# Attention over grouped heads: moving the softmax division from ACT's output pass to POOL

One change to a tuned attention kernel: the division by the softmax row sum, which ScalarE (ACT) did while it took the output out of PSUM, is done later by GpSimd (POOL), from an f32 copy in SBUF. VectorE (DVE) computes the reciprocals for four tiles of 128 rows at a time, and the order of the matmuls on TensorE (PE) changes.

## The chip, the core and the metric

The kernel runs on one core of a Trainium2 chip. The metric is the device time of one execution in microseconds (us). In both kernels PE multiplies and transposes into the memory PSUM, ACT and DVE read PSUM, POOL reads and writes the memory SBUF only, and SP issues the DMAs.

## The reference

```python
B, Hq, Hkv, Sq, Sk, D = 16, 16, 8, 384, 384, 256      # bf16
k = jnp.repeat(k, 2, axis=1); v = jnp.repeat(v, 2, axis=1)
scores = jnp.einsum("bhqd,bhkd->bhqk", q, k) * D ** -0.5
p = softmax(scores, axis=-1)
out = jnp.einsum("bhqk,bhkd->bhqd", p, v)
```

## The kernel before

An *item* is 128 query rows of one key/value head. There are 768 of them, 12 to a *group* (two key/value heads of one batch entry, one set of loads and one store). For each item:

| step | engine | what it does |
|---|---|---|
| S | PE | 2 matmuls, 384 columns: scores into PSUM |
| max | DVE | row maximum of the scores, negated |
| exp | ACT | exp(score - max), bf16, to SBUF |
| T | PE | 3 transposes of 128x128 |
| copy | DVE | transposed weights from PSUM to SBUF |
| PV | PE | 3 matmuls, 257 columns: V has a column of ones, so column 257 is the row sum |
| recip | DVE | 1 / row sum |
| output | ACT | output x reciprocal, bf16, to SBUF |

POOL scales K once for each group. A planner gives every instruction a place in the order of its engine and a semaphore wait for each dependence. The places are set by offsets from a step number `y`. The code is shortened: `...` and the comments in the last loop stand for lines left out.

```python
    A_S = 2            # scores run two items ahead
    D_PV = 2           # PV follows two items later
    D_REC = 3; D_OE = 3
    NSB = 4; NWB = 4   # PSUM banks for scores, and for transposes + output
    ...
        def mk_oe(x):                                   # ACT's output pass
            g, u, t = item_gut(x)
            def emit(eng):
                return eng.activation(
                    out=O_sb[g % NOS][:, u, t, :], in_=O_ps(x)[:, 0:D], func=ACTF.Identity,
                    scale=recip[:, (x % NREC):(x % NREC) + 1])
            return emit
    ...
                    o = pl.add("sp", f"ldkt{g % NGS}", mk_load_kt(g), deps, dma=True, ...)
                    ks = pl.add("pool", "pool_ks", mk_kscale(g), [o], ...)   # at once after the load
    ...
        for y in range(y_min, y_max + 1):
            try_loads(y)
            # x = y + A_S:  pl.add("pe",  ... mk_s(x))
            # x = y - D_PV: pl.add("pe",  ... mk_pv(x))
            # x = y - D_REC: pl.add("dve", ... mk_recip(x))
            # x = y - 1:    pl.add("dve", ... mk_pte(x))     the copy
            # x = y + 2:    pl.add("dve", ... mk_max(x))
            # x = y:        pl.add("act", ... mk_exp(x)); pl.add("pe", ... mk_t(x))
            # x = y - D_OE: pl.add("act", ... mk_oe(x)); store after the last item of a group
```

Of the kernel before, what the change touches and what calls it, by code (L numbers as in the profile page):

```python
# [88 lines left out]
def bass_standalone__gqa_softmax__near_ridge_kernel(  # L89
# [12 lines left out]
    assert Sk * 4 <= 2048, "S tile must fit in one PSUM bank"  # L102
    PT_BYTES = JK * 128 * 2
    assert PT_BYTES % 4 == 0 and PT_BYTES + (D + 1) * 4 <= 2048, "PT + O tile must fit one PSUM bank"
    scale = float(D) ** -0.5
# [9 lines left out]
    NWB = 4  # L115
    A_S = 2
    D_PV = 2
    D_T = 0
    D_REC = 3
    D_PTE = 1  # L120
    A_MAX = 2
    D_OE = 3
    NGS = 4
    NOS = 4
    PF = 20
    NP, NPT, NNEG, NREC = 4, 4, 8, 8
    SPLIT_GROUPS = 2
# [5 lines left out]
    def grp_bk(g):  # L133
        U0 = g * GU
        return U0 // Hkv, U0 % Hkv

    with ExitStack() as es:
        def sb(name, shape, dtype):
            return es.enter_context(nc.sbuf_tensor(name, shape, dtype))

        def ps(name, shape, dtype):
            return es.enter_context(nc.psum_tensor(name, shape, dtype))

# [6 lines left out]
        P_sb = [sb(f"P_sb{i}", [128, Sk], BF16) for i in range(NP)]  # L150
        PT_sb = [sb(f"PT_sb{i}", [128, JK, 128], BF16) for i in range(NPT)]
        negm = sb("negm", [128, NNEG], F32)
        recip = sb("recip", [128, NREC], F32)

        S_ps = [ps(f"S_ps{i}", [128, Sk], F32) for i in range(NSB)]
        W_ps = [ps(f"W_ps{i}", [128, 1024], BF16) for i in range(NWB)]

        def PT_ps(x):
            return W_ps[x % NWB][:, 0:JK * 128].rearrange("p (c n) -> p c n", c=JK)

        def O_ps(x):
            e0 = PT_BYTES // 2
            return W_ps[x % NWB][:, e0:e0 + 2 * (D + 1)].bitcast(F32)

# [10 lines left out]
        def G(key):  # L175
            return ops.get(key)

        def item_gut(x):
            g = x // IPG
            u = (x % IPG) // IPU  # L180
            t = x % IPU
            return g, u, t

        def emit_ones(eng):
# [7 lines left out]
        def mk_vones(i):  # L192
            def emit(eng):
                return eng.memset(V_sb[i][:, :, :, D:D + 1], 1.0)  # L194
            return emit

        def mk_load_kt(g, u0=0, nu=None):
# [49 lines left out]
        def mk_kscale(g, u0=0, nu=None):  # L247
            nu = GU if nu is None else nu

            def emit(eng):  # L250
                kt = KT_sb[g % NGS][:, :, u0 * 128:(u0 + nu) * 128]
                return eng.tensor_scalar(out=kt, in0=kt, scalar1=scale, scalar2=0.0,  # L252
                                         op0=ALU.mult, op1=ALU.add)
            return emit

        def mk_s(x):
            g, u, t = item_gut(x)

            def emit(eng):
                last = None  # L260
                for dc in range(DC):
                    last = eng.matmul(  # L262
                        out=S_ps[x % NSB][:, :],
                        lhsT=QT_sb[g % NGS][:, DC * t + dc, u * 128:(u + 1) * 128],
                        rhs=KT_sb[g % NGS][:, dc:JK * DC:DC, u * 128:(u + 1) * 128],
                        start=(dc == 0), stop=(dc == DC - 1))
                return last
            return emit

        def mk_max(x):  # L270
            def emit(eng):
                return eng.tensor_reduce(  # L272
                    out=negm[:, (x % NNEG):(x % NNEG) + 1], in_=S_ps[x % NSB][:, :],
                    axis=AXL.X, op=ALU.max, negate=True)
            return emit

        def mk_exp(x):
            def emit(eng):
                return eng.activation(  # L279
                    out=P_sb[x % NP][:, :], in_=S_ps[x % NSB][:, :], func=ACTF.Exp,  # L280
                    bias=negm[:, (x % NNEG):(x % NNEG) + 1], scale=1.0)
            return emit

        def mk_t(x):
            def emit(eng):
                last = None
                for kc in range(JK):
                    last = eng.transpose(  # L288
                        out=PT_ps(x)[:, kc, :],
                        in_=P_sb[x % NP][:, kc * 128:(kc + 1) * 128],  # L290
                        identity=ident[:])
                return last
            return emit
# [19 lines left out]

        def mk_recip(x):
            def emit(eng):
                return eng.reciprocal(out=recip[:, (x % NREC):(x % NREC) + 1],  # L316
                                      in_=O_ps(x)[:, D:D + 1])
            return emit

        def mk_oe(x):  # L320
            g, u, t = item_gut(x)

            def emit(eng):
                return eng.activation(  # L324
                    out=O_sb[g % NOS][:, u, t, :], in_=O_ps(x)[:, 0:D], func=ACTF.Identity,
                    scale=recip[:, (x % NREC):(x % NREC) + 1])
            return emit

        def emit_warm(eng):
            last = None  # L330
            for i in range(N_WARM):
                last = eng.matmul(out=S_ps[NSB - 1][:, 0:128], lhsT=ident[:], rhs=ident[:],  # L332
                                  start=True, stop=True)
            return last

# [7 lines left out]
        def last_item_of_group(g):  # L343
            return g * IPG + IPG - 1

        next_load = [0]

        def try_loads(y):
            while next_load[0] < NG:
                g = next_load[0]  # L350
                if y < g * IPG - A_S - PF:
                    return
# [23 lines left out]
                else:  # L376
                    o = pl.add("sp", f"ldkt{g % NGS}", mk_load_kt(g), deps, dma=True, name=f"ldkt{g}")
                    ks = pl.add("pool", "pool_ks", mk_kscale(g), [o], name=f"kscale{g}")
                    o = pl.add("sp", f"ldqt{g % NGS}", mk_load_qt(g), deps, dma=True, name=f"ldqt{g}")
                    for u in range(GU):  # L380
                        ops[("kscale", g, u)] = ks
                        for t in range(IPU):
                            ops[("ldqt", g, u, t)] = o
                    for u in range(GU):
                        ops[("ldv", g, u)] = pl.add("sp", f"ldv{g % NGS}_{u}", mk_load_v(g, u), vdeps, dma=True, name=f"ldv{g}_{u}")
                next_load[0] += 1

        y_min = -A_S - PF
        y_max = NI - 1 + max(D_OE, D_PV, D_T, D_REC, D_PTE) + 1
        for y in range(y_min, y_max + 1):  # L390
            try_loads(y)

            x = y + A_S
            if 0 <= x < NI:
                g, u, t = item_gut(x)
                deps = [ops[("ldqt", g, u, t)], ops[("kscale", g, u)], (G(("exp", x - NSB)), "order"), G("warm")]
                ops[("s", x)] = pl.add("pe", "pe_s", mk_s(x), deps, name=f"s{x}")
            x = y - D_PV
            if 0 <= x < NI:
                g, u, t = item_gut(x)  # L400
                deps = [ops[("pte", x)], ops[("ldv", g, u)]]
                ops[("pv", x)] = pl.add("pe", "pe_pv", mk_pv(x), deps, name=f"pv{x}")

            x = y - D_REC
            if 0 <= x < NI:
                deps = [ops[("pv", x)], (G(("oe", x - NREC)), "order")]
                ops[("recip", x)] = pl.add("dve", "dve_recip", mk_recip(x), deps, name=f"recip{x}")
            x = y - D_PTE
# [12 lines left out]

            x = y - D_T
            if 0 <= x < NI:
                deps = [ops[("exp", x)], (G(("oe", x - NWB)), "order"), ops["ident"]]
                ops[("t", x)] = pl.add("pe", "pe_t", mk_t(x), deps, name=f"t{x}")

            x = y - D_OE
            if 0 <= x < NI:
                g = x // IPG
                deps = [ops[("pv", x)], ops[("recip", x)], (G(("store", g - NOS)), "order")]  # L430
                ops[("oe", x)] = pl.add("act", "act_oe", mk_oe(x), deps, name=f"oe{x}")
                gg, u, t = item_gut(x)
                for pi, (u0, nu, t0, nt) in enumerate(store_pieces(g)):
                    if u == u0 + nu - 1 and t == t0 + nt - 1:
                        deps = [ops[("oe", g * IPG + uu * IPU + tt)]
                                for uu in range(u0, u0 + nu) for tt in range(t0, t0 + nt)]
                        chan = f"st{g % NOS}" if pi == 0 else f"st_last{pi}"
                        o = pl.add("sp", chan, mk_store(g, u0, nu, t0, nt), deps, dma=True, name=f"store{g}_{pi}")
                        if pi == 0:
                            ops[("store", g)] = o  # L440

        for x in range(NI):
            for kname in ("s", "max", "exp", "t", "pte", "pv", "recip", "oe"):
                assert (kname, x) in ops, (kname, x)
# [67 lines left out]
```

## Time and profile before

| | before |
|---|---|
| time, median of 4 | 656.96 us (656.9 to 657.67) |
| span of the profiled execution | 655.2 us |
| time per item in steady state (end of exp to end of exp) | 836.8 ns |
| start of the last exp to the end of the span | 5.1 us |

The first fence holds lines of the profile page of the kernel before: the busy time of each engine with its share of the span, and the chain of waits that ended last. SPq is SP's sequencer, which issues the DMAs, and "issue" is time in which an engine waited for nothing that the profile shows.

```profile
PE 647.8 (99%) x6180; PEld 448.6 (68%) x6180; DVE 643.0 (98%) x2308; ACT 644.8 (98%) x1537; POOL 95.3 (15%) x72
...
ACT 92%; issue 3%; SPq 3%; DMA 1%; PE 0%; DVE 0%
```

Three engines are 98 to 99% busy, so the busy shares don't say which of them sets the pace. The next lines are the costliest groups of the same page. The columns are source line, engine, operation, output<-inputs, shapes and count, then total busy us and mean ns of one, then idle time before it and what ended it.

```profile
L279 ACT ACTIVATE P_sb<-S_ps,negm 128x384 bf16<-128x384 f32 x768 | 542.6, 707 | 5.8 <-DVE negm L272 5.6
L324 ACT ACTIVATE O_sb<-W_ps,recip 128x256 bf16<-128x256 f32 x768 | 465.9, 607 | 1.6 <-DVE recip L316 1.6
L272 DVE TENSOR_REDUCE negm<-S_ps 128x1 f32<-128x384 f32 x768 | 428.3, 558 | 7.4 <-PE S_ps L262 7.3
L297 DVE COPY PT_sb<-W_ps 128x384 bf16<-128x384 bf16 x768 | 259.9, 338 | 0.7 <-PE W_ps L288 0.7
```

The two ACT records together are 1,314 ns for an item that takes 837 ns. Records of one engine overlap: an instruction's record opens while the one before it is still running. So a mean duration is not what an instruction costs its engine, and the distances between instructions must be read. The timeline of ACT in steady state (start us, duration us, engine, line, operation):

```profile
300.40 0.71 ACT L279 ACTIVATE P_sb<-S_ps,negm 128x384 bf16<-128x384 f32 x1
300.86 0.61 ACT L324 ACTIVATE O_sb<-W_ps,recip 128x256 bf16<-128x256 f32 x1
301.23 0.71 ACT L279 ACTIVATE P_sb<-S_ps,negm 128x384 bf16<-128x384 f32 x1
```

From exp to output pass 0.46 us, back to exp 0.37 us. PE at two times, first early in the run (13 us), then in steady state:

```profile
13.00 0.33 PE L288 MATMUL W_ps<-ident,P_sb 128*128 128x128 bf16 x3
13.16 0.49 PE L262 MATMUL S_ps<-KT_sb,QT_sb 128*128 128x384 bf16 x2
13.49 0.50 PE L306 MATMUL W_ps<-V_sb,PT_sb 128*128 128x257 bf16 x3
13.82 0.33 PE L288 MATMUL W_ps<-ident,P_sb 128*128 128x128 bf16 x3
...
300.33 0.34 PE L288 MATMUL W_ps<-ident,P_sb 128*128 128x128 bf16 x3
300.50 0.49 PE L262 MATMUL S_ps<-KT_sb,QT_sb 128*128 128x384 bf16 x2
300.83 0.50 PE L306 MATMUL W_ps<-V_sb,PT_sb 128*128 128x257 bf16 x3
301.16 0.34 PE L288 MATMUL W_ps<-ident,P_sb 128*128 128x128 bf16 x3
```

Early on, an item takes 827 ns and every matmul follows the one before at once. Later it takes 837 ns, and the transposes begin 56 ns after exp has ended (at 301.11: 300.40 + 0.71), item after item. In between, exp's records grow by about 10 ns per item. ACT is the slower of the two, by that much; when a load stall has let it catch up, PE shows its own pace for some 15 items.

### The profile page before, as it was taken

The page shows a single profiled execution, that of the slowest core. Times are in us where ns is not written, and L with a number is a line of the kernel's source. Part 1 is how long each engine was busy: PE and PEld are TensorE (multiplying, and loading weights), DVE is VectorE, ACT ScalarE, POOL GpSimd, SP SyncE. Part 2 cuts the span into 40 slices and gives each one's busy share as a digit, 9 for nine tenths or more (in the row PEclk, how much of TensorE's full clock was granted, in tenths as well). Part 3 has the DMA queues.
Part 4 walks back from the last instruction along what each step waited for, and adds up shares of the span by engine and source line. Part 5 has one row for each costly group of instructions (what it writes and reads, how often), then busy time and mean ns, then how long its engine had stood idle before and what let it go on. Part 6 is the DMA issues. An engine that isn't in the chain of part 4 may idle for free.

```text
span 655.2 us, 16888 instructions
## 1 busy us (share of the span) xinstructions
PE 647.8 (99%) x6180; PEld 448.6 (68%) x6180; DVE 643.0 (98%) x2308; ACT 644.8 (98%) x1537; POOL 95.3 (15%) x72
## 2 busy tenths in 40 slices
PE   7999999999999999999999999999999999999997
PEld 6777666666666666666666666666666666666665
DVE  5999999999999999999999999999999999999997
ACT  5999999999999999999999999999999999999998
POOL 1111111101101101101111110110110111101100
PEclk9999999999999999999999999999999999999999
DMA  8999999999999999999999999999999999999932
GB/s 153 171 256 221 254 258 241 261 253 258 214 245 248 232 244 250 218 262 250 230 251 255 233 258 250 246 233 253 243 237 235 227 253 221 227 249 247 225 126 98
DMA packets 368019, 152.11 MB, mean 232 GB/s; under 512 B 302272, under 2 KB 351680, under 8 KB 367936
## 3 DMA queue, kind: packets, MB, share of 16 engines
q1 hardware_dynamic: 367936, 151.02, 104.2%
q8 instruction: 49, 0.80, 0.5%
q14 instruction: 34, 0.28, 0.2%
HBM read 25.17 MB, written 50.33 MB: 115 GB/s over the span
## 4 chain that ended last, share of the span: by engine, by line
ACT 92%; issue 3%; SPq 3%; DMA 1%; PE 0%; DVE 0%
ACT P_sb L279 54%; ACT O_sb L324 38%; SPq L203 1%; SPq L214 1%; DMA QT_sb<-in_q_dram 1%; SPq L223 0%; DVE negm L272 0%; PE W_ps L306 0%; PE S_ps L262 0%; DVE PT_sb L297 0%; PE W_ps L288 0%; DVE recip L316 0%
## 5 line engine op out<-in xcount | busy, mean ns | idle before, releaser
L279 ACT ACTIVATE P_sb<-S_ps,negm 128x384 bf16<-128x384 f32 x768 | 542.6, 707 | 5.8 <-DVE negm L272 5.6
L324 ACT ACTIVATE O_sb<-W_ps,recip 128x256 bf16<-128x256 f32 x768 | 465.9, 607 | 1.6 <-DVE recip L316 1.6
L272 DVE TENSOR_REDUCE negm<-S_ps 128x1 f32<-128x384 f32 x768 | 428.3, 558 | 7.4 <-PE S_ps L262 7.3
L306 PE MATMUL W_ps<-V_sb,PT_sb 128*128 128x257 bf16 x2304 | 382.4, 274 | 0.1
L262 PE MATMUL S_ps<-KT_sb,QT_sb 128*128 128x384 bf16 x1536 | 375.1, 326 | 2.1 <-DMA QT_sb<-in_q_dram 1.9
L306 PEld LDWEIGHTS W_ps<-V_sb,PT_sb 128*128 128x128 bf16 x2304 | 226.2, 98 | 108.5 <-DVE PT_sb L297 0.4
L297 DVE COPY PT_sb<-W_ps 128x384 bf16<-128x384 bf16 x768 | 259.9, 338 | 0.7 <-PE W_ps L288 0.7
L288 PE MATMUL W_ps<-ident,P_sb 128*128 128x128 bf16 x2304 | 259.3, 221 | 0.8 <-ACT P_sb L279 0.8
L288 PEld LDWEIGHTS W_ps<-ident,P_sb 128*128 128x128 bf16 x2304 | 132.8, 97 | 90.0 <-ACT P_sb L279 1.7
L252 POOL TENSOR_SCALAR KT_sb<-KT_sb 128x1536 bf16<-128x1536 bf16 (+1 forms) x66 | 94.6, 1434 | 526.1 <-DMA KT_sb<-in_k_dram 526.1
L316 DVE RECIPROCAL recip<-W_ps 128x1 f32<-128x1 f32 x768 | 121.2, 158 | 0.5 <-PE W_ps L306 0.5
L262 PEld LDWEIGHTS S_ps<-KT_sb,QT_sb 128*128 128x128 bf16 x1536 | 117.9, 98 | 3.4 <-DMA QT_sb<-in_q_dram 2.9
L332 PE MATMUL S_ps<-ident 128*128 128x128 bf16 x36 | 4.0, 310 | 1.4 <-POOL ident L188 1.4
L332 PEld LDWEIGHTS S_ps<-ident 128*128 128x128 bf16 x36 | 3.8, 145 | 1.4 <-POOL ident L188 1.4
L279 ACT ACT_TABLE_LOAD x1 | 1.3, 1283 | 0.8 <-PEq L497 0.8
L194 DVE MEMSET V_sb<- 128x6 bf16 x4 | 0.2, 63 | 0.9 <-PEq L497 0.9
L188 POOL TENSOR_SCALAR_AFFINE_SELECT ident<-ones_t 128x128 bf16<-128x128 bf16 x1 | 0.3, 293 | 0.1
L185 POOL MEMSET ones_t<- 128x128 bf16 x1 | 0.2, 205 | 0.3 <-POOLq L497 0.3
L497 POOL MEMSET const-float32-0.0<- 128x1 f32 x1 | 0.1, 99 | 0.3 <-issue 0.3
L497 POOL MEMSET const-bfloat16-1.0<- 128x1 bf16 x1 | 0.1, 102 | 0.0
L497 POOL MEMSET const-uint8-127<- 128x1 uint8 x1 | 0.1, 102 | 0.0
L497 POOL MEMSET const-float32-1.0<- 128x1 f32 x1 | 0.1, 99 | 0.0
## 6 DMA issues: line engine op xcount, KB each, us to landing
out_dram<-O_sb SPq DMA_DIRECT2D x63, 768.0 KB, 5.2
V_sb<-in_v_dram SPq DMA_DIRECT2D x128, 192.0 KB, 3.5
QT_sb<-in_q_dram SPq DMA_TRANSPOSE x67, 7.1
KT_sb<-in_k_dram SPq DMA_TRANSPOSE x66, 6.2
out_dram<-O_sb SPq DMA_DIRECT2D x1, 384.0 KB, 2.6
out_dram<-O_sb SPq DMA_DIRECT2D x2, 192.0 KB, 1.8
```

Source lines behind the costliest of these rows:

```text
L203: return eng.dma_start_transpose(out=KT_sb[g % NGS][:, :, u0 * 128:(u0 + nu) * 128], in_=src)
L214: return eng.dma_start_transpose(out=QT_sb[g % NGS][:, t0 * DC:(t0 + nt) * DC, u0 * 128:(u0 + nu) * 128], in_=src)
L252: return eng.tensor_scalar(out=kt, in0=kt, scalar1=scale, scalar2=0.0, op0=ALU.mult, op1=ALU.add)
L262: last = eng.matmul(out=S_ps[x % NSB][:, :], lhsT=QT_sb[g % NGS][:, DC * t + dc, u * 128:(u + 1) * 128], rhs=KT_sb[g % NGS][:, dc:JK * DC: ...
L272: return eng.tensor_reduce(out=negm[:, (x % NNEG):(x % NNEG) + 1], in_=S_ps[x % NSB][:, :], axis=AXL.X, op=ALU.max, negate=True)
L279: return eng.activation(out=P_sb[x % NP][:, :], in_=S_ps[x % NSB][:, :], func=ACTF.Exp, bias=negm[:, (x % NNEG):(x % NNEG) + 1], scale=1.0)
L288: last = eng.transpose(out=PT_ps(x)[:, kc, :], in_=P_sb[x % NP][:, kc * 128:(kc + 1) * 128], identity=ident[:])
L297: return eng.tensor_copy(out=PT_sb[x % NPT][:, :, :], in_=PT_ps(x))
L306: last = eng.matmul(out=O_ps(x), lhsT=PT_sb[x % NPT][:, kc, :], rhs=V_sb[g % NGS][:, u, kc, :], start=(kc == 0), stop=(kc == JK - 1))
L316: return eng.reciprocal(out=recip[:, (x % NREC):(x % NREC) + 1], in_=O_ps(x)[:, D:D + 1])
L324: return eng.activation(out=O_sb[g % NOS][:, u, t, :], in_=O_ps(x)[:, 0:D], func=ACTF.Identity, scale=recip[:, (x % NREC):(x % NREC) + 1])
L332: last = eng.matmul(out=S_ps[NSB - 1][:, 0:128], lhsT=ident[:], rhs=ident[:], start=True, stop=True)
```

## The change

Its intent: take work off ACT by letting POOL, 15% busy, do the division. ACT copies the output from PSUM to an f32 scratch in SBUF (12 slots), and POOL scales it from there. With the change, PSUM is declared as one tensor, so `S_ps` and `W_ps` both appear as `PS`. The core of the diff, with cuts marked:

```diff
-    A_S = 2
+    A_S = 3
+    RB = 4            # reciprocals in batches of four items
+    KS_LEAD = 10      # K scaling enters POOL's order 10 items before its first use
+    NO32 = 12
 ...
+        O32 = sb("O32", [128, NO32, D + 1], F32)
 ...
-        def mk_oe(x): ... activation(out=O_sb[...], in_=O_ps(x)[:, 0:D], func=Identity, scale=recip[...])
+        def mk_oev(x, engname): ... activation(out=O32[:, x % NO32, :], in_=O_ps(x), func=Identity)
+        def mk_recipb(x0, n): ... reciprocal(out=recip[:, r0:r0 + n], in_=O32[:, s0:s0 + n, D])
+        def mk_norm(x): ... tensor_scalar(out=O_sb[...], in0=O32[:, x % NO32, 0:D],
+                                          scalar1=recip[...], scalar2=0.0, op0=mult, op1=add)   # POOL
 ...
-                    ks = pl.add("pool", "pool_ks", mk_kscale(g), [o], name=f"kscale{g}")
+                    pending_ks[g] = o          # scaled later, by try_kscales(y), from the third group on
 ...
+            try_kscales(y)
+            # PE's order in a step is now PV(y-2), S(y+3), T(y); before: S(y+2), PV(y-2), T(y)
 ...
+                if x % RB == RB - 1 or x == NI - 1:
+                    rb = pl.add("dve", ..., mk_recipb(x0, n), ...)
+                    for xx in range(x0, x + 1):
+                        ops[("norm", xx)] = pl.add("pool", "pool_norm", mk_norm(xx), ...)
```

## The prediction

> **What bounds it now.** The page's busy shares (PE 99%, ACT 98%, DVE 98%) don't decide it; the chain of waits gives ACT 92%. In the timeline one item (128 query rows) takes 836.7 ns in steady state, and ACT sets it: exp start to output-scaling start 464 ns, back to exp 372 ns. The transposes start 56 ns after exp's end, every time, and one gap between transposes is 63 ns instead of 55.
> After each load stall early on, PE shows its own pace: items 46 to 60 pass at 827 ns with all eight matmuls back to back (55+55+55+163+162+110+114+112). There exp's records grow by 10 ns per item, 582 to 712 ns, until ACT has fallen behind and takes over. So ACT is slower than PE by only 9.7 ns per item. The Trainium skill, "TensorE: Matmul & The Clock Gate", Back-to-back issue gap, gives N/2.4 + 2.5 ns: 821 ns for these eight, near the 827.
> DVE runs 475 (reduce) + 75 (reciprocal) + 277 to 287 (copy), in step with the others.
>
> **What the change does.**
> - ACT's output pass loses its per-row scale (a pointer operand) and the wait for the reciprocal; it writes 257 f32 elements instead of 256 bf16. The skill, "ScalarE: Activation LUTs", What ACT_TABLE_LOAD costs, counts about 93 ns per pointer operand; no trace yet shows it. The two passes' fixed parts (464 - 384 x 0.833 = 144, 372 - 256 x 0.833 = 159 ns) suggest that most may be hidden: I expect ACT at 740 to 825 ns per item.
> - DVE does one reciprocal per four items: about 770.
> - POOL gets 768 normalisations. From the K scaling (1473 ns for 1536 elements, 832 for 768: 0.834 ns each plus 192) I estimate 405 ns each: POOL 95 to 406 us, 63% busy, not binding. The scratch's 12 slots last 10 us; a batch needs about 3.
> - PE's eight matmuls stay, in the order PV, S, transposes; scores run three items ahead.
> - DMA moves the same bytes. SP waited 74 us for outputs, so later stores have room.
>
> **On the critical path.** ACT can give only 9.7 ns per item before PE binds. About 70 of 768 items already ran at 827, so the gain is 698 x 9.7 ns = 6.8 us. The tail grows: after the last output pass come a reciprocal and four normalisations, about +1.6 us. One more score product before the first transpose: +0.2 us. 656.96 - 6.8 + 1.6 + 0.2 = 651.8 us, 0.8% faster; range 648.5 to 658.5. Chances: faster by over 2% 0.03 (643.8 us would need under 817 ns per item, below PE's pace); within 2% 0.88; slower 0.09.
>
> **What would show it.** Right: exp start to start 827 ns, PE back to back, transposes no longer 56 ns after exp's end, the chain of waits on PE; exp's records shorter than 712 ns; DVE idle; POOL 55 to 70% busy, normalisations near 405 ns; the last 1.5 us on POOL. Wrong in ACT's size: cadence stays at 836 with exp at 712 ns (about 658 us). Wrong in POOL: normalisations over 700 ns, ACT waiting for POOL.
>
> **What would make it wrong.** A POOL normalisation far dearer (f32 input, pointer scalar), or slowed by DVE on shared SBUF ports; the f32 write slowing ACT; DVE's reciprocal, which now waits for ACT, holding up the copies behind it; K scaling queued behind normalisations making PE wait; the new matmul order moving PE by a few ns per item.

## The result

| | before | after |
|---|---|---|
| time, median | 656.95 us (15 runs) | 652.36 us (10 runs, 651.1 to 654.19) |
| ratio | | 0.9928, 95% interval 0.9919 to 0.9937 |
| per item, steady state | 836.8 ns | 827.1 ns |
| start of the last exp to the end of the span | 5.1 us | 6.8 us |
| span of the profiled execution | 655.2 us | 653.4 us |

Ratios here and below are the mean time of one kernel's fast runs over that of the kernel before in the same rounds, so they are not quite the ratio of the medians quoted. The profiled execution of the kernel after was its slowest (655.13 us); a second profile further down is nearer to the median.

The same parts of the page, after:

```profile
PE 642.3 (98%) x6180; PEld 506.6 (78%) x6180; DVE 632.7 (97%) x1732; ACT 637.1 (98%) x1537; POOL 450.0 (69%) x840
...
DVE 93%; SPq 3%; DMA 1%; PE 1%; issue 1%; POOL 0%; POOLq 0%
...
L350 POOL TENSOR_SCALAR O_sb<-O,recip 128x256 bf16<-128x256 f32 x768 | 354.7, 483 | 177.3 <-DVE recip L343 171.7
L296 ACT ACTIVATE P_sb<-PS,negm 128x384 bf16<-128x384 f32 x768 | 446.3, 581 | 6.2 <-DVE negm L289 5.8
L289 DVE TENSOR_REDUCE negm<-PS 128x1 f32<-128x384 f32 x768 | 420.6, 548 | 6.2 <-PE PS L279 6.2
L334 ACT ACTIVATE O<-PS 128x257 f32<-128x257 f32 x768 | 290.1, 378 | 4.8 <-PE PS L322 4.7
L313 DVE COPY PT_sb<-PS 128x384 bf16<-128x384 bf16 x768 | 274.7, 358 | 8.3 <-PE PS L305 5.5
```

ACT's records have shrunk from 707 to 581 ns (exp) and from 607 to 378 ns (output): nothing queues up on ACT any more. But its busy share is 98% as before, since records that abut or overlap leave no gap to be counted. The chain of waits now names DVE with 93%. PE and DVE in steady state, after:

```profile
300.13 0.49 PE L279 MATMUL PS<-KT_sb,QT_sb 128*128 128x384 bf16 x2
300.45 0.33 PE L305 MATMUL PS<-ident,P_sb 128*128 128x128 bf16 x3
300.62 0.50 PE L322 MATMUL PS<-V_sb,PT_sb 128*128 128x257 bf16 x3
300.95 0.49 PE L279 MATMUL PS<-KT_sb,QT_sb 128*128 128x384 bf16 x2
```
```profile
299.90 0.17 DVE L343 RECIPROCAL recip<-O 128x4 f32<-128x4 f32 x1
299.99 0.36 DVE L313 COPY PT_sb<-PS 128x384 bf16<-128x384 bf16 x1
300.26 0.55 DVE L289 TENSOR_REDUCE negm<-PS 128x1 f32<-128x384 f32 x1
300.82 0.36 DVE L313 COPY PT_sb<-PS 128x384 bf16<-128x384 bf16 x1
301.09 0.55 DVE L289 TENSOR_REDUCE negm<-PS 128x1 f32<-128x384 f32 x1
```

PE's matmuls stand as close as they did early in the kernel before: 162+162+56+56+56+110+114+112 = 828 ns by the medians of the distances. The transposes now begin 675 ns after exp has ended (median), so PE no longer waits for ACT. DVE starts the copy 0.55 us after the reduce, whether a reciprocal stands between them (0.46 + 0.09) or not. So in three items of four DVE has room that the page doesn't show. That contradicts the chain's verdict, and the experiments decide it.

The end of the run, POOL's last line:

```profile
649.26 1.84 POOL L350 TENSOR_SCALAR O_sb<-O,recip 128x256 bf16<-128x256 f32 x4 [0.41 <-DVE recip L343]
```

The last four items are scaled one after another, 1.84 us, before the last store can go.

### The profile page after: what moved, and what is told of

It is laid out like the page before. It is cut to its first block, busy times and chain, and to the rows that moved or that the text cites. A ratio compares the mean times of both kernels' runs of the same rounds, so it can differ in the third digit from the quotient of the medians.

```text
span 653.4 us, 17836 instructions
## 1 busy us (share of the span) xinstructions
PE 642.3 (98%) x6180; PEld 506.6 (78%) x6180; DVE 632.7 (97%) x1732; ACT 637.1 (98%) x1537; POOL 450.0 (69%) x840
## 4 chain that ended last, share of the span: by engine, by line
DVE 93%; SPq 3%; DMA 1%; PE 1%; issue 1%; POOL 0%; POOLq 0%
DVE negm L289 53%; DVE PT_sb L313 38%; DVE recip L343 2%; DMA QT_sb<-in_q_dram 1%; SPq L231 1%; SPq L220 1%; POOL O_sb L350 0%; SPq L240 0%; PE PS L279 0%; PE PS L322 0%; PE PS L305 0%; POOLq L502 0%
## 5 line engine op out<-in xcount | busy, mean ns | idle before, releaser
L350 POOL TENSOR_SCALAR O_sb<-O,recip 128x256 bf16<-128x256 f32 x768 | 354.7, 483 | 177.3 <-DVE recip L343 171.7
L296 ACT ACTIVATE P_sb<-PS,negm 128x384 bf16<-128x384 f32 x768 | 446.3, 581 | 6.2 <-DVE negm L289 5.8
L289 DVE TENSOR_REDUCE negm<-PS 128x1 f32<-128x384 f32 x768 | 420.6, 548 | 6.2 <-PE PS L279 6.2
L322 PE MATMUL PS<-V_sb,PT_sb 128*128 128x257 bf16 x2304 | 383.1, 275 | 0.2
L279 PE MATMUL PS<-KT_sb,QT_sb 128*128 128x384 bf16 x1536 | 373.9, 325 | 4.6 <-DMA QT_sb<-in_q_dram 4.3
L334 ACT ACTIVATE O<-PS 128x257 f32<-128x257 f32 x768 | 290.1, 378 | 4.8 <-PE PS L322 4.7
L313 DVE COPY PT_sb<-PS 128x384 bf16<-128x384 bf16 x768 | 274.7, 358 | 8.3 <-PE PS L305 5.5
L305 PEld LDWEIGHTS PS<-ident,P_sb 128*128 128x128 bf16 x2304 | 192.0, 97 | 101.2 <-issue 0.7
L305 PE MATMUL PS<-ident,P_sb 128*128 128x128 bf16 x2304 | 254.1, 219 | 0.1
L322 PEld LDWEIGHTS PS<-V_sb,PT_sb 128*128 128x128 bf16 x2304 | 194.3, 98 | 10.2 <-DVE PT_sb L313 0.6
```

What stands on the lines that cost most here:

```text
L279: last = eng.matmul(out=S_ps(x)[:, :], lhsT=QT_sb[g % NGS][:, DC * t + dc, u * 128:(u + 1) * 128], rhs=KT_sb[g % NGS][:, dc:JK * DC:DC, u ...
L289: return eng.tensor_reduce(out=negm[:, (x % NNEG):(x % NNEG) + 1], in_=S_ps(x)[:, :], axis=AXL.X, op=ALU.max, negate=True)
L296: return eng.activation(out=P_sb[x % NP][:, :], in_=S_ps(x)[:, :], func=ACTF.Exp, bias=negm[:, (x % NNEG):(x % NNEG) + 1], scale=1.0)
L305: last = eng.transpose(out=PT_ps(x)[:, kc, :], in_=P_sb[x % NP][:, kc * 128:(kc + 1) * 128], identity=ident[:])
L313: return eng.tensor_copy(out=PT_sb[x % NPT][:, :, :], in_=PT_ps(x))
L322: last = eng.matmul(out=O_ps(x), lhsT=PT_sb[x % NPT][:, kc, :], rhs=V_sb[g % NGS][:, u, kc, :], start=(kc == 0), stop=(kc == JK - 1))
```

## Experiments

The theory: ACT bound the kernel before, by the cost of one pointer operand (here `scale=recip[...]`: a scale that the instruction reads from SBUF, one value for each row); taking it away uncovers PE, 9.7 ns per item further on, and the rest of ACT's relief is lost because PE is then back to back. Rivals: the gain came from the wait for the reciprocal, from the new matmul order or from the batching; or the kernel after is bound by DVE, as its chain of waits says. The twelve runs (eleven edited kernels and the kernel after once more) came with runs of the kernel before: experiments 1 to 3 (chip 8, median of before 656.56 us), 5 to 7 and the split of 8 (chip 8, 655.18 us), 4, 9, 10 and the early scaling of 8 (chip 0, 655.37 us). So times in us shift by up to 1.8 us, and four expected ranges were undercut by 0.7 to 1.4 us (experiments 1, 5, 6 and 7); the ratios to before are what can be compared.

### 1. The pointer alone, taken away

```diff
 # kernel before
-    in_=O_ps(x)[:, 0:D], func=ACTF.Identity, scale=recip[:, ...])
+    in_=O_ps(x)[:, 0:D], func=ACTF.Identity)
```

> The kernel before, with the scale pointer taken off ACT's output pass and nothing else (the reciprocal is still computed and still waited for; 256 bf16 elements to the same place). The result is wrong on purpose: rows are not normalised. Theory (the pointer operand is what costs ACT its 9.7 ns too many): ACT falls below PE's pace, items pass at 827 ns, exp's records shrink from 712 to about 580 ns, time 650 to 651 us. Rival (the wait for the reciprocal, or the PSUM read of the row sum by DVE, is what held ACT): stays at 836.7 ns and 657 us.

Measured: 649.27 us against 656.56, ratio 0.9887 (0.9872 to 0.9901); 827.1 ns per item. The result was wrong, as intended. The ACT groups of its page:

```profile
L279 ACT ACTIVATE P_sb<-S_ps,negm 128x384 bf16<-128x384 f32 x768 | 442.1, 576 | 5.7 <-DVE negm L272 5.6
L324 ACT ACTIVATE O_sb<-W_ps 128x256 bf16<-128x256 f32 x768 | 295.2, 384 | 1.8 <-DVE recip L316 1.8
```

The same instruction without `recip` among its inputs has a record of 384 ns instead of 607, and the whole steady gain of the change is there, although the reciprocal is still computed for each item and still waited for. It is even faster than the change; it doesn't have the longer tail, which experiment 7 prices at about 1.5 us. It is no kernel one can use.

### 2. The pointer put back into the kernel after

```diff
 # kernel after; one_f is a [128, 1] column of ones
-    return eng.activation(out=dst, in_=O_ps(x), func=ACTF.Identity)
+    return eng.activation(out=dst, in_=O_ps(x), func=ACTF.Identity, scale=one_f[:, 0:1])
```

> The kernel after, with a scale pointer (a column of ones) put back on ACT's output pass; the result stays right. Theory of the pointer: items pass at 836 to 837 ns again, exp's records grow to about 710 ns, time 658 to 660 us (slower than the kernel before, because the longer tail stays). Rival (the gain came from the reciprocal's wait, the new matmul order or the batched reciprocal): stays at 827 ns and 652 us.

Measured: 659.27 us, ratio 1.0041 (1.0024 to 1.0058), correct; 837.8 ns per item.

```profile
L298 ACT ACTIVATE P_sb<-PS,negm 128x384 bf16<-128x384 f32 x768 | 638.4, 1174 | 5.7 <-DVE negm L291 5.5
L336 ACT ACTIVATE O<-PS,one_f 128x257 f32<-128x257 f32 x768 | 634.6, 1070 | 0.9 <-PE PS L324 0.7
```

The gain is gone, and the records have grown to 1,174 and 1,070 ns: work queues on ACT again, here more deeply than before. The chain of waits on the page of this run still names DVE, although the pointer on ACT is all that was put back and the transposes again begin 56 ns after exp has ended:

```profile
DVE 93%; ACT 2%; issue 2%; POOL 1%; SPq 1%; DMA 1%; PE 0%; POOLq 0%
```

With this run the chain view is known to be wrong for this kernel.

### 3. PE relieved, after and before

```diff
 # both kernels: the third of three PV matmuls left out (wrong result)
-    for kc in range(JK):
+    for kc in range(JK - 1):
```

> The kernel after with the third of the three output matmuls left out (wrong on purpose): PE loses 110 to 114 ns per item, nothing else changes. Theory (PE binds the kernel after): the item falls to the next floor, which I expect at 750 to 800 ns, set by DVE (475 + 275 + a quarter of 87 = 772) or ACT; time 605 to 630 us. Rival (DVE binds, as the chain of waits says with its 93%): stays at 827 ns and 652 us.

> The kernel before with the same matmul left out (wrong on purpose). Theory (ACT binds the kernel before, by 9.7 ns): nothing is gained, 836 to 837 ns per item, 656.5 to 658 us. Rival (PE binds or all three are in lockstep): faster by tens of us.

Measured: the kernel after falls to 619.73 us (ratio 0.9444, 0.9419 to 0.9468), the kernel before stays at 656.66 us (0.9997, 0.9982 to 1.0012). So PE's work sets the time of the kernel after and not that of the kernel before. Between stalls an item took 747 ns (end of exp to end of exp, median); over the whole run 787 ns, as the engines now stand still between such stretches: PE waited 29.1 us for Q's load, in 31 waits. That the loads are the next wall is read from these waits; no run tests it.

### 4. ACT's own floor

```diff
 # kernel after: the third chunk left out of T, copy and PV (wrong result)
-    for kc in range(JK):             # transposes, and PV
+    for kc in range(JK - 1):
-    eng.tensor_copy(out=PT_sb[x % NPT][:, :, :], in_=PT_ps(x))
+    eng.tensor_copy(out=PT_sb[x % NPT][:, 0:JK - 1, :], in_=PT_ps(x)[:, 0:JK - 1, :])
```

> The kernel after with the third chunk left out of transposes, copy and output product (wrong on purpose): PE loses 168 ns and DVE about 66 ns per item, ACT keeps all its work. It measures ACT's own floor. Between load stalls ACT should pass an item in 725 to 750 ns (465 + 265 back to back was seen with one matmul less), so about 90 ns below 836.7, which is what the trace of one pointer operand should cost; load stalls (DMA) will keep the whole near 610 to 620 us. Rival (the pointer costs little and ACT is near 825): 815 to 825 ns between stalls.

Measured: 613.24 us (a single execution, its state unknown). A stretch of ACT's timeline without a stall:

```profile
421.78 0.79 ACT L296 ACTIVATE P_sb<-PS,negm 128x384 bf16<-128x384 f32 x1
422.25 0.60 ACT L334 ACTIVATE O<-PS 128x257 f32<-128x257 f32 x1
422.51 0.80 ACT L296 ACTIVATE P_sb<-PS,negm 128x384 bf16<-128x384 f32 x1
422.97 0.61 ACT L334 ACTIVATE O<-PS 128x257 f32<-128x257 f32 x1
423.24 0.82 ACT L296 ACTIVATE P_sb<-PS,negm 128x384 bf16<-128x384 f32 x1
```

Starts come every 0.73 us, but each record is longer than the last by 18 ns: the ends come every 745 ns (5th to 95th percentile of the queued items 744 to 746). That is ACT's floor without the pointer. With it (experiment 2, same 257 f32 elements) it is 837.8. The pointer operand costs 837.8 - 745 = 93 ns, of which the change could use only 9.7. The two runs come from different chips; against the 747 ns of experiment 3, it is 91. The Trainium skill, "ScalarE: Activation LUTs", What ACT_TABLE_LOAD costs, says that each [128,1] pointer operand adds about 93 ns; this agrees, with 91 to 93.

### 5. DVE loaded again

```diff
 # kernel after
-    RB = 4
+    RB = 1
```

> The kernel after with one reciprocal for each item instead of one for each four; the result stays right. DVE gets 0.75 x 88 = 66 ns more per item. Theory (PE binds, and DVE has about 75 ns of unseen room in three items of four, since the copy starts 552 ns after the reduce with or without a reciprocal between them): still 827 to 829 ns per item, and the tail loses three normalisations of 0.45 us: 651 to 652 us. Rival (DVE binds, as the chain of waits says): 890 ns per item and about 700 us.

Measured: 649.66 us, ratio 0.9915 (0.9902 to 0.9929), correct; 827.1 ns per item. DVE's timeline:

```profile
300.14 0.55 DVE L289 TENSOR_REDUCE negm<-PS 128x1 f32<-128x384 f32 x1
300.61 0.15 DVE L343 RECIPROCAL recip<-O 128x1 f32<-128x1 f32 x1
300.70 0.36 DVE L313 COPY PT_sb<-PS 128x384 bf16<-128x384 bf16 x1
300.97 0.55 DVE L289 TENSOR_REDUCE negm<-PS 128x1 f32<-128x384 f32 x1
```

Every item now has its reciprocal and the item is not longer by a nanosecond. DVE does not bind the kernel after, and the batching contributes nothing to its steady state. It costs a little at the end instead: the start of the last exp to the end of the span is 5.5 us here and 6.8 in the kernel after.

### 6. The matmul order alone

```diff
 # kernel before
-    A_S = 2          # order S, PV, T
+    A_S = 3          # order PV, S, T
```

> The kernel before with the matmul order of the kernel after (output product, then scores three items ahead, then transposes) and nothing else. Theory (order does nothing while ACT binds): 836.7 ns per item, 656.5 to 658 us. Rival (the order gave part of the gain): 650 to 655 us.

Measured: 655.61 us, ratio 1.0004 (0.9991 to 1.0017), correct; 835.0 ns per item in its profile. The order is not what gained. Its profile shows 1.8 ns per item less than 836.8, with no shorter time than the kernel before had. But the kernel before itself was 1.4 us faster there than in the call before, about what 1.8 ns in each of 768 items would give. Whether the order made this difference stays open.

### 7. The tail

```diff
 # kernel after: the last four items as in the kernel before
+            if NI - RB <= x < NI:
+                r = pl.add("dve", "dve_recip", mk_recip1(x), ...)   # from PSUM
+                o = pl.add("act", "act_oev", mk_oe1(x), ...)        # scales, writes O_sb
```

> The kernel after with the last four items normalised as in the kernel before (reciprocal from PSUM on DVE, scaling pass on ACT), so that nothing of them passes through POOL. Theory (the longer tail costs 1.7 us: 6.81 us from the last exp to the end against 5.09 before): 1.5 to 2 us faster than the kernel after, 650.4 to 651 us, cadence unchanged. Rival (the tail is hidden by the store): no change, 652.4 us.

Measured: 649.36 us, ratio 0.9911 (0.9898 to 0.9925), correct; 827.1 ns per item; 5.3 us from the start of the last exp to the end, 1.5 less than the kernel after. The unchanged kernel after had 650.85 us, ratio 0.9937, on another chip (experiment 9); the ratios differ by 0.0026, or 1.7 us. The tail costs about what its time says. With experiment 5, from which it can't be told apart (0.9911 and 0.9915), this is the fastest correct kernel.

### 8. Two tries at the start that failed, and what they showed

```diff
 # kernel after, first try: third group's loads split by unit (one key/value head), too
-    SPLIT_GROUPS = 2
+    SPLIT_GROUPS = 3
 # kernel after, second try: K scaling at once after its load, as in the kernel before
-    KS_LEAD = 10
+    KS_LEAD = 20
```

> The kernel after with the third group's K and Q loads also split by unit, as those of the first two groups are. Theory (the start loses 1 to 3 us to the third group's Q load, on which PE stood 2.3 us at 26.5 us in the profiled run): 1 to 2 us faster than the kernel after and less scattered, 650.5 to 651.5 us. Rival (the loads at the start are bound by what the DMA queue can move, not by when the first unit lands): no change.

> The kernel after with the K scaling put into POOL's order as soon as its load is issued (20 items ahead instead of 10), as the kernel before has it. Theory (POOL is in order and now also has the normalisations; a K scaling that waits for its load at the start holds them up, the scratch's 12 slots fill, and ACT, then PE, stand still, as the run with the third group split showed by 6.5 us): 655 to 668 us, with ACT waiting for POOL near 20 to 40 us and no change of the 827 ns later. Rival (POOL has so much room that the place of the K scaling doesn't matter): 652 us.

Measured: 659.41 us (1.0059, 1.0045 to 1.0073) and 661.19 us (1.0105, 1.0089 to 1.0122), both correct, both slower. The first expectation was wrong; the second gave the time, but not where the waits fall. From the waits of the two runs (who waited for whom: us in total, times, longest us), first that of the split, then that of the early scaling:

```profile
ACT O L334 <- POOL O_sb L350: 7.0, 1, 7.0
```
```profile
POOL KT_sb L269 <- DMA KT_sb<-in_k_dram: 194.2, 66, 4.7
ACT O L334 <- POOL O_sb L350: 10.8, 9, 3.9
```

In a split group the K scaling goes into POOL's order as soon as the load is issued, so POOL stood waiting for K while finished outputs waited behind it; the 12 slots filled and ACT waited 7.0 us for POOL. The second run does the same to every group, and ACT waits nine times: once 3.9 us at 21 to 25 us, as expected, but then eight times more, 6.9 us in all, between 82 and 513 us. In the kernel before, which has the early scaling, POOL waited 526 us for K at no cost, because nothing stood behind the scaling. `KS_LEAD` is therefore the part of the change without which it would be slower than the kernel before: by 1% instead of 0.7% faster.

### 9. The kernel after once more

> The kernel after, unchanged, so that the other runs of this call have it on the same chip. 0.992 to 0.994 of the kernel before, 827 ns per item; its start (the first 48 items) shows whether the 2.3 us stand of PE at 26.5 us in the first profile comes each time: I expect less of it, as the profiled run was the slowest of its kind (655.13 against a median of 652.36).

Measured: 650.85 us, ratio 0.9937 (0.9925 to 0.995); 827.1 ns per item. The first 48 items took 851 ns each, against 939 in the first profile, where PE stood 2.3 us for the third group's Q, and 872 in the kernel before. So the start differs between executions, and the change doesn't make it worse each time.

### 10. A try at PE's own work

```diff
 # the kernel of experiment 7, row sums from exp, PV without its column of ones (cut: the reciprocals read rsum)
-    bias=negm[...], scale=1.0)
+    bias=negm[...], scale=1.0, accum_out=rsum[:, (x % NREC):(x % NREC) + 1])
-    rhs=V_sb[g % NGS][:, u, kc, :],
+    rhs=V_sb[g % NGS][:, u, kc, 0:D],
```

> A version meant to beat both: the kernel after with the short tail of the run a_tail, and with the row sums taken from exp's accumulator output on ACT instead of a 257th column of the output product (three matmuls of 256 columns instead of 257). The result stays right. Theory (only PE's own work moves the item now): 827.1 - 3 x 0.42 = 825.9 ns, 1 us less than a_tail, 0.989 to 0.990 of the kernel before. Rival (the accumulator's read-out costs ACT more than its 83 ns of room): over 830 ns per item, slower than the kernel after.

Measured: 655.47 us, ratio 1.0004 (0.9992 to 1.0017), correct; 835.1 ns per item. The rival held.

```profile
L297 ACT ACTIVATE P_sb<-PS,negm 128x384 bf16<-128x384 f32 x768 | 633.5, 1089 | 6.5 <-DVE negm L290 6.3
L336 ACT ACTIVATE O<-PS 128x256 f32<-128x256 f32 x764 | 619.9, 885 | 0.0
L297 ACT ACTIVATION_READ_ACCUMULATOR P_sb<-PS,negm 128x1 f32 x768 | 539.7, 703 | 0.0
```

The accumulator output is a second instruction on ACT, and ACT's item rises from 745 to 835 ns, about 90 ns more; there were only 82 ns of room below PE's 827. Again ACT's records queue up, and all that the pointer had freed is spent.

## Why the prediction was right

Predicted 651.8 us, 5.1 less than before; measured 652.36, 4.6 less. The steady state was to give 6.8 us, and from item 60 to item 760 the two profiles give (836.75 - 827.14) x 700 = 6.7 us; the tail takes about 1.8 of it back. That the time fits to 0.6 us is in part luck, as the same kernel had 650.85 us later. Point by point:

- *ACT binds before, by 9.7 ns:* shown. Leaving out a PV matmul changes nothing before (experiment 3), and the pointer alone brings 827.1 ns (experiment 1).
- *PE's own pace, 827 ns, is the next wall:* shown by the relief of PE (experiment 3) and by loading DVE without effect (experiment 5). It was legible in the profile of before, in the items after each load stall. The Trainium skill, "TensorE: Matmul & The Clock Gate", Back-to-back issue gap, gives N/2.4 + 2.5 ns for the isolated gap of one matmul, which makes an estimate of 821 ns for these eight; the trace has 6 ns more, some of it in the PV matmuls (112 ns on average for 109.6). For a stream of weight loads and matmuls, which this is, the section expects about 81 ns each at 128 columns; the transposes here took 56, so that figure does not hold.
- *Most of the pointer's 93 ns may be hidden, ACT at 740 to 825 ns:* the floor is 745, inside the range, but the reasoning was wrong. Nothing is hidden: the pointer costs its full 91 to 93 ns. I had split start-to-start distances into a fixed part for each pass, and start stamps don't carry that. It did no harm since ACT was off the critical path either way.
- *The tail, +1.6 us:* 6.8 instead of 5.1 us, +1.7, from the start of the last exp; from its end 6.2 instead of 4.4, +1.9. Experiment 7 takes most of it back.
- *POOL, 405 ns per normalisation and 63% busy:* 453 ns from one to the next, records of 483 ns, 69% busy. The estimate from the K scaling was 11% low, and POOL is not on the critical path. DVE did not slow POOL visibly: the last normalisations, after DVE has finished, are 453 to 455 ns apart, and those beside a working DVE 453 to 456. The skill, "SBUF — State Buffer", Who interferes with whom, says that a DVE instruction with at most one SBUF input does not contend with GpSimd outside the 2-port modes. The reduce and the copy here read PSUM and have no SBUF input, and the trace agrees; whether the copy runs in such a mode no run shows.
- *The chain of waits on PE, DVE idle:* wrong as signs. The chain says DVE 93% and DVE's busy share is 97%. DVE's records of one item, 548 + 358 = 906 ns, are longer than the item, so no idle time is left to see, and the chain, which stays on an engine without gaps, stays there. The same chain stood in experiment 2, where ACT bound.
- *K scaling queued behind normalisations:* named as a risk. The real hazard is the opposite order, normalisations behind a K scaling that waits for its load; `KS_LEAD` had already dealt with it (experiment 8).

## What to carry to other kernels

When three engines are all 98% busy, find the places where one of them has just caught up, after a stall: the others show their own pace there, and the difference is all that relief of the bound engine can bring. Here ACT was freed of over 90 ns per item and the time fell by under 10, because PE came next at 827; with PE relieved, the items took 787 on average, with waits for loads. When an idle in-order engine is given a second job, look at what its first job waits for: waits that cost nothing become waits of the second job.

## What the Trainium skill lacked or had wrong

- "Perfetto Trace Analysis", Per-instruction lifecycle, puts the start of a DVE or ACT record at the moment when its ALUs begin. The same instruction's records grow here by 18 ns per item, with starts 727 and ends 745 ns apart (experiment 4), so the start of a queued ACT instruction seems to come before that. Ends give the engine's pace, and a growing record shows which engine falls behind.
- "ScalarE: Activation LUTs" mentions an accumulator output without its price: a separate instruction in the trace, and about 90 ns more per ACT item (745 to 835 ns, experiments 4 and 10).
- The same page's 93 ns per pointer operand is right, and, which the page leaves open, it is time of the engine in a queued stream, not latency alone (745 against 837.8 ns).
- "GPSIMD Engine Reference" has no figure for a POOL `tensor_scalar` with a pointer operand: 453 to 456 ns from one to the next for 128x256 f32 to bf16. The records of the K scaling with constants (832 ns for 768 columns, 1,473 for 1,536) would make it 405 ns, an estimate.
- "Perfetto Trace Analysis", Identifying the Most-Contended Engine, calls occupancy a fair measure for ACT and DVE. Here ACT's was 98% in the kernel it bound and 98% in the kernel that PE bound, with 82 ns of each 827 free.
